# State tiles in one plane, gates' second part on GpSimd, a lag between pairs, and a new order, in an mLSTM and two-MoE kernel

## The chip, the cores and the metric

One core of a Trainium2 chip runs the whole program in one launch. The metric is the device time of one execution in microseconds (us). The engines are TensorE (PE, with its weight loads as PEld), VectorE (DVE), ScalarE (ACT), GpSimd (POOL) and SyncE (SP), which issues the DMAs.

## What is computed

```python
for t in range(S):                       # B=2, H=8, S=768, D=40
    m_new = np.maximum(f_gate[:, :, t] + m, i_gate[:, :, t])
    f_stab = np.exp(f_gate[:, :, t] + m - m_new)
    i_stab = np.exp(i_gate[:, :, t] - m_new)
    C = f_stab[..., None, None] * C + i_stab[..., None, None] * np.einsum('bhd,bhe->bhde', vt, kt)
    n = f_stab[..., None] * n + i_stab[..., None] * kt
    y[:, :, t] = sigmoid(o_gate) * einsum('bhde,bhe->bhd', C, qt) / maximum(abs(n . qt), 1)
x = y as (1536, 320)
h = x @ w_in                             # 320 -> 2048
g = (a0 + a1 h + a2 h^2 + a3 h^3) / (1 + |b0||h| + |b1|h^2 + 1e-6)
x = g @ w_out                            # 2048 -> 320
xn = x / rms(x) * rms_g
out = (silu(xn @ w_gate) * (xn @ w_val)) @ w_out2    # 320 -> 1536 -> 320
```

The weights arrive as 64-bit floats and are converted on the chip.

## The kernel before

**Recurrence.** The 2 x 768 tokens are 12 chunks of 128 (chunk j: batch j // 6). A chunk's tasks on TensorE are s (L504, K^T Q by head, tiles of 64 rows by 128 columns), f (L484, the forget factors spread over partitions), yi (L527, the state times Q, for chunks that aren't the first of their batch), y (L537, the inner part), u (L549, the update of the state) and xt (L645, three transposes). In yi one matmul takes both heads of a pair: 128 rows of Q against a state `cst` in two planes, whose other half is zero, so that 82 columns stream past 64 weight columns. On VectorE stand two scans (L487), two products a (L509), ys (L531) and yd (L541), ca (L563, two pieces, one for each half of the partitions) and xl (L653); on GpSimd vp, v2, cd (L555, two pieces), rs and xm.

**Gates.** They are worked out in two parts, steps 0 to 255 and 256 to 767: gm (L423, a scan), ga (L430, L431) and gi (L434, on GpSimd), gb (two ScalarE instructions), gc, gd (L449, scans whose second operand is a zero column `zc`) and ge (transposes to `idt`). f of a chunk needs gc of its part; the products a need ge.

**First MoE.** A pair i is 256 hidden units (weight group p) of 256 tokens (block n): `PAIRS[i] = (n, p)`. Its tasks are in0 and in1 (L676, 8 matmuls each), a chain over ScalarE, GpSimd and VectorE that ends in g (L739), and out0 and out1 (L681 for the first 16 pairs, in four-pass float32; L695 and L697 after that). Blocks 0 and 1 go together, p by p. in0 of block n needs xl of chunks 2n and 2n + 1. A weight group is loaded, converted on VectorE in halves (c0 L331, c1 L337, c2 L343, or c2 on GpSimd with a carry on ScalarE), then split by hi (L360) and its low words (L364).

**Second MoE.** From about 320 us gate and value products (L865) and output sums (L873 to L875) fill TensorE.

**Order.** All is divided into some 1,950 tasks with dependencies and buffers from rings (eight PSUM banks are the ring "b"). The table ORDER lists the tasks' numbers in the order in which they are issued; it was made elsewhere, and every engine runs its instructions in that order. A table entry moved moves all that its task issues, DMAs too.

```python
def run():
    for x in ORDER:
        key, fn, deps, take, give = tasks[x]
        for tag, name in take:
            held[name] = (tag, rings[tag].pop(0))
        if fn: fn()
        for name in give: ...      # buffer back to its ring
```

## Time and profile before

| | |
|---|---|
| three runs | 484.04 us median (482.48 to 484.82) |
| the profiled execution | 483.95 us, span 482.18 us |
| PE / PEld busy | 459.9 us (95%) / 416.2 us (86%) |
| DVE, ACT, POOL busy | 333.4 us (69%), 305.3 us (63%), 316.7 us (66%) |
| first and last matmul start | 8.14 us, 478.5 us |
| DMA | 40.4 MB, mean 84 GB/s |

The span reaches from the first to the last instruction; the launch around it is in the execution's own time. A busy share is an average over stages. Matmuls are pipelined, so the length that a row of the timeline gives reaches beyond the next row's start; what a task costs is read from its start to the next row's start. In the timeline equal instructions that follow each other are one row with a count, and a float32 matmul shows as two instructions.

### The profile page before, as it was taken

Reading aid. Unit: us, or ns where it says so; the run is one execution under the profiler, and the core shown is the slowest. Engines: PE = TensorE matmul, PEld = TensorE weight load, DVE = VectorE, ACT = ScalarE, POOL = GpSimd, SP = SyncE. Lnnn points to the kernel's source line nnn. Section 1 sums busy time; section 2 is a strip of 40 time slices with the busy share of each in tenths; the row PEclk is TensorE's granted clock in tenths of the full one; section 3 lists DMA queues with packets and bytes.
Section 4 is the critical chain, followed back from the end, with each engine's and each line's share of the span. In section 5 each row is a group of like instructions: output and inputs, shape, how many; then the busy total and the mean of one; then the engine's idle time right before and its main releaser. Section 6 shows DMA issues by size and latency. Waiting matters only on the chain.

```text
...
## 1 busy us (share of the span) xinstructions
PE 459.9 (95%) x3552; PEld 416.2 (86%) x3552; DVE 333.4 (69%) x609; ACT 305.3 (63%) x576; POOL 316.7 (66%) x337
## 2 busy tenths in 40 slices
...
GB/s 249 256 171 283 48 179 114 165 56 115 2 15 89 34 114 50 28 2 84 33 142 57 94 98 190 225 153 72 1 1 14 88 0 2 27 42 1 1 1 56
DMA packets 18366, 40.41 MB, mean 84 GB/s; under 512 B 3952, under 2 KB 11904, under 8 KB 18320
## 3 DMA queue, kind: packets, MB, share of 16 engines
...
q8 instruction: 28, 0.46, 0.4%
q14 instruction: 18, 0.15, 0.1%
...
## 4 chain that ended last, share of the span: by engine, by line
PE 59%; ACT 13%; DVE 13%; POOL 10%; issue 4%; DMA 1%; POOLq 0%; DVEq 0%; ACTq 0%
PE bank L865 24%; PE bank L676 9%; PE bank L695 5%; PE bank L873 4%; PE bank L875 4%; PE bank L874 4%; PE bank L697 2%; POOL win L364 2%; ACT z L710 2%; PE bank L681 1%; DVE vv L727 1%; POOL scr L356 1%; DVE bank L737 1%; POOL z L720 1%; DVE vv L739 1%
## 5 line engine op out<-in xcount | busy, mean ns | idle before, releaser
L676 PE MATMUL bank<-xall,win 128*128 128x256 f32 x768 | 104.1, 290 | 2.4 <-DVE vv L739 0.8
L676 PEld LDWEIGHTS bank<-xall,win 128*128 128x128 f32 x768 | 97.0, 194 | 6.8 <-DVE xall L653 1.0
L941 DVE TENSOR_TENSOR vv<-bank,vv 128x512 f32<-128x512 f32 x35 | 24.1, 690 | 103.4 <-PE bank L865 84.5
L720 POOL TENSOR_TENSOR z<-z,u 128x512 f32<-128x512 f32 x48 | 62.2, 1295 | 11.7 <-ACT z L710 10.7
L947 POOL TENSOR_TENSOR wou<-vv,wou 128x512 fp32r<-128x512 f32 x12 | 15.5, 1296 | 50.8 <-ACT wou L944 50.7
L938 ACT ACTIVATE vv<-bank 128x512 f32<-128x512 f32 x35 | 20.6, 594 | 42.4 <-PE bank L865 38.9
L865 PE MATMUL bank<-xall,w2gv 128*128 128x512 f32 (+1 forms) x256 | 46.9, 338 | 0.3 <-ACT vv L938 0.3
L749 POOL TENSOR_TENSOR gl<-vv,gh 128x512 fp32r<-128x512 f32 x32 | 41.6, 1300 | 7.6 <-ACT gh L748 5.1
L865 PEld LDWEIGHTS bank<-xall,w2gv 128*128 128x128 f32 x256 | 39.3, 190 | 5.5 <-ACT vv L938 0.8
L710 ACT ACTIVATE z<-u,few 128x512 f32<-128x512 f32 x48 | 39.0, 813 | 1.7 <-DVE vv L739 0.6
L681 PE MATMUL bank<-scr,vv 128*128 128x320 f32 x128 | 38.0, 439 | 1.5 <-DVE vv L739 1.2
L695 PE MATMUL bank<-wou,gh 128*128 128x320 f32 x128 | 39.1, 317 | 0.1
L697 PE MATMUL bank<-wou,gh 128*128 128x320 f32 x128 | 38.0, 309 | 0.0
L737 DVE SCALAR_TENSOR_TENSOR bank<-vv,few,bank 128x512 f32<-128x512 f32 x48 | 35.8, 747 | 0.0
L735 DVE SCALAR_TENSOR_TENSOR z<-z,bank 128x512 f32<-128x512 f32 x48 | 32.6, 680 | 3.9 <-ACT bank L734 3.0
L732 ACT ACTIVATE bank<-z,few 128x512 f32<-128x512 f32 x48 | 32.7, 682 | 1.1 <-POOL z L720 0.6
L739 DVE SCALAR_TENSOR_TENSOR vv<-z,bank 128x512 f32<-128x512 f32 x48 | 32.7, 681 | 0.6
L947 POOL TENSOR_TENSOR gl<-vv,wou 128x512 fp32r<-128x512 f32 x11 | 14.2, 1296 | 28.0 <-ACT wou L944 17.1
L331 DVE TENSOR_SCALAR bank<-raw 128x320 int32<-128x320 int32 x68 | 32.4, 484 | 0.1
L681 PEld LDWEIGHTS bank<-scr,vv 128*128 128x128 f32 x128 | 22.9, 190 | 11.0 <-DVE vv L739 2.3
L947 POOL TENSOR_TENSOR wou<-vv,gh 128x512 fp32r<-128x512 f32 x10 | 12.9, 1299 | 29.1 <-ACT gh L944 28.9
L865 PE MATMUL bank<-win,w2gv 128*128 128x512 f32 x128 | 30.7, 390 | 0.0
...
## 6 DMA issues: line engine op xcount, KB each, us to landing
...
```

Of the source, the lines that this page charges most:

```text
L676: PE.matmul(out=hb()[:, e], lhsT=l, rhs=r, start=(x == 0), stop=(x == len(mm) - 1))
L681: PE.matmul(out=T("acc", n, t)[:, 0:DM], lhsT=T("vv", i)[:, e, t * 128:(t + 1) * 128], rhs=w[:, e], start=p + e == 0, stop=p == NPAIR - 1 ...
L695: PE.matmul(out=o, lhsT=l, rhs=woh[:, e], start=first, stop=last)
L697: PE.matmul(out=o, lhsT=l, rhs=wol[:, e], start=False, stop=False)
L710: go("z", lambda: ACT.activation(out=z(), in_=u(), func=ACTF.Identity, scale=babs[:, 1:2], bias=babs[:, 0:1]), [("hu", i)], ["z"])
L720: go("zu", lambda: POOL.tensor_tensor(out=z(), in0=z(), in1=u(), op=ALU.mult), [("z", i)], [], ["u"])
L732: go("ars", lambda: ACT.activation(out=hb(), in_=z(), func=ACTF.Abs_reciprocal_sqrt, bias=cq), [("zu", i), ("p3", i)])
L737: go("y2", lambda: DVE.scalar_tensor_tensor(out=hb(), in0=vv(), scalar=nacoef[:, 0:1], in1=hb(), op0=ALU.add, op1=ALU.mult), [("w", i)])
L739: go("g", lambda: DVE.scalar_tensor_tensor(out=vv(), in0=z(), scalar=2.0, in1=hb(), op0=ALU.subtract, op1=ALU.mult), [("y2", i)], [], ["z" ...
L749: go("gl", lambda: POOL.tensor_tensor(out=gl(), in0=vv(), in1=r32(gh()), op=ALU.subtract), [("gh", i)], ["gl"], ["vv"])
L865: PE.matmul(out=bank(i, e), lhsT=l, rhs=r, start=y == 0, stop=y == len(mm) - 1)
L947: task(("sl",) + k2, lambda: POOL.tensor_tensor(out=flat("sl", *k2), in0=flat("sg", *k2), in1=r32(flat("sh", *k2)), op=ALU.subtract), [("s ...
```

## The change

The state `cst` has one plane. yi takes 16 matmuls of 40 rows by 64 columns (tiles 64x64, at four places of the array) into two banks, one for the even and one for the odd heads, and ys reads them in two pieces. u loads 64 columns of K for each head (40 of the head and 24 that follow; the last head's are zero), so that it writes all 128 partitions, and ca and cd are one piece each. The zeros of `lqk` and `cst` are no longer written at the start. ga and gi are one task: for the first part on VectorE (three instructions), for the second on GpSimd (three instructions). `zc` is a column of the PSUM bank that ge uses. Pairs of block 1 follow those of block 0 one weight group later. ORDER is another table; the diff shows its first line in each kernel, and the rows behind the diff what moved.

```diff
--- before.py
+++ after.py
@@ -20,101 +20,102 @@
 OB = [["ob"] * 4, ["raw", "raw", "raw", "ob"], ["ob", "raw"], ["ob", "cv"]]
 F_CV = [1] * 16 + [0] * 18
 NATIVE = [0, 1, 2, 3, 4, 5, 6, 7, 8, 9, 10, 11, 12, 13, 14, 15]
+LAG = 1
 BY_SQUARE = [0, 2, 4, 6, 8, 10, 12, 14, 16, 18, 20, 22, 24, 26, 28]
 ORDER = [
-    0, 374, 379, 8, 10, 19, 375, 9, 11, 21, 393, 20, 22, 36, 376, 377, 394, 12, 13, 2, 3, 17, 23, 94, 378, 28, 30,
...
+    0, 8, 9, 10, 18, 11, 391, 392, 396, 12, 372, 373, 375, 393, 394, 1, 13, 374, 376, 34, 19, 20, 395, 21, 377, 15,
...
 ]
 
 
@@ -162,7 +163,8 @@
 
     BLOCKS = [(0, 2 * BLK), (2 * BLK, 2 * BLK), (4 * BLK, BLK), (5 * BLK, BLK)]
 
-    PAIRS = [(n, p) for p in range(NPAIR) for n in range(2)] + [(n, p) for n in range(2, NB) for p in range(NPAIR)]
+    PAIRS = [(n, x - n * LAG) for x in range(NPAIR + LAG) for n in range(2) if 0 <= x - n * LAG < NPAIR]
+    PAIRS += [(n, p) for n in range(2, NB) for p in range(NPAIR)]
     FINAL = [max(i for i, x in enumerate(PAIRS) if x[0] == n) for n in range(NB)]
 
     PE, ACT, DVE, POOL = nc.tensor, nc.scalar, nc.vector, nc.gpsimd
@@ -265,13 +267,12 @@
     dexp = at.tile([48, NCH, BH // 2], FP32, name="dexp")
     idt = at.tile([128, NCH, 48], FP32, name="idt")
     dl = at.tile([128, NCH, BH // 2], FP32, name="dl")
-    cst = at.tile([128, HP, 2, D1], FP32, name="cst")
-    zc = at.tile([48, 1], FP32, name="zc")
+    cst = at.tile([128, HP, D1], FP32, name="cst")
     den = at.tile([128, H, 1], FP32, name="den")
-    for nm, n in (("k", 2), ("v", 2)):
-        ring("l" + nm, tiles(at, n, [128, H, D], FP32, "l" + nm))
-    qk_bufs = tiles(at, 2, [128, 2, HP, L], FP32, "lqk")
-    ring("lqk", qk_bufs)
+    ring("lv", tiles(at, 2, [128, H, D], FP32, "lv"))
+    lk_bufs = tiles(at, 2, [128, H * D + 64 - D], FP32, "lk")
+    ring("lk", lk_bufs)
+    ring("lqk", tiles(at, 2, [128, 2, HP, L], FP32, "lqk"))
     ring("yb", tiles(at, 2, [128, H, D1], FP32, "yb"))
 
 
@@ -282,7 +283,10 @@
     def load(i, nm):
         if nm != "qk":
             src = {"k": k, "v": v, "o": o_gate}[nm][i * L:(i + 1) * L].rearrange("p (h d) -> p h d", h=H)
-            nc.sync.dma_start(out=lo_of(i) if nm == "o" else T("l" + nm, i), in_=src)
+            dst = lo_of(i) if nm == "o" else T("l" + nm, i)
+            if nm == "k":
+                dst = dst[:, 0:H * D].rearrange("p (h d) -> p h d", h=H)
+            nc.sync.dma_start(out=dst, in_=src)
             return
         for e in range(2):
             nc.sync.dma_start(
@@ -403,11 +407,8 @@
         DVE.memset(g48, 0.0)
         DVE.memset(cq, 1.0 + 1e-6)
         DVE.memset(eps6, 1e-6)
-        POOL.memset(zc, 0.0)
-        for t in qk_bufs:
-            for r0 in (32, 96):
-                POOL.memset(t[r0:r0 + 32, 0], 0.0)
-        POOL.memset(cst, 0.0)
+        for t in lk_bufs:
+            POOL.memset(t[:, H * D:], 0.0)
         for nm, dst, src in (
             ("eye", ident, eye4[:, 0:128]), ("eye4", id4, eye4), ("sel", sel, pick), ("hv", hv[FR], halves),
             ("pb", bcoef, pb[None, :].to_broadcast([128, 2])), ("pa", acoef, pa[None, :].to_broadcast([128, 4])),
@@ -426,12 +427,11 @@
         )
 
     def gate_a(a, b):
-        gf = gate_in[:, 0, a:b]
-        DVE.tensor_tensor(out=gf, in0=gf, in1=m_t[:, a:b], op=ALU.add)
-        DVE.tensor_tensor(out=g48[FR, a:b], in0=gf, in1=m_t[:, a + 1:b + 1], op=ALU.subtract)
-
-    def gate_i(a, b):
-        POOL.tensor_tensor(out=g48[0:BH, a:b], in0=gate_in[:, 1, a:b], in1=m_t[:, a + 1:b + 1], op=ALU.subtract)
+        e = POOL if a else DVE
+        gf, m1 = gate_in[:, 0, a:b], m_t[:, a + 1:b + 1]
+        e.tensor_tensor(out=gf, in0=gf, in1=m_t[:, a:b], op=ALU.add)
+        e.tensor_tensor(out=g48[FR, a:b], in0=gf, in1=m1, op=ALU.subtract)
+        e.tensor_tensor(out=g48[0:BH, a:b], in0=gate_in[:, 1, a:b], in1=m1, op=ALU.subtract)
 
     def gate_b(a, b):
         ACT.activation(out=g48[:, a:b], in_=g48[:, a:b], func=ACTF.Exp)
@@ -444,9 +444,11 @@
         DVE.memset(f16[:, a:b].rearrange("p (c l) -> p c l", l=L)[:, :, 0:1], 0.0)
 
     def gate_d(a, b):
+        zc = T("gt", a)[FR, 511:512]
+        DVE.memset(zc, 0.0)
         for c in range(a // L, b // L):
             sl = g48[FR, c * L:(c + 1) * L]
-            DVE.tensor_tensor_scan(out=sl, data0=sl, data1=zc[FR].to_broadcast([BH, L]), initial=1.0, op0=ALU.mult, op1=ALU.add)
+            DVE.tensor_tensor_scan(out=sl, data0=sl, data1=zc.to_broadcast([BH, L]), initial=1.0, op0=ALU.mult, op1=ALU.add)
 
     def gate_e(a, b):
         c0, c1 = a // L, b // L
@@ -521,14 +523,22 @@
             return T(name, j)[:, 0:H * D1].rearrange("p (h d) -> p h d", h=H)
 
         def yi():
-            t = heads("pi")
             for p in range(HP):
                 for c in (slice(0, 64), slice(64, 128)):
-                    PE.matmul(out=t[c, 2 * p:2 * p + 2], lhsT=T("lqk", j)[:, 0, p, c], rhs=cst[:, p])
+                    for e in range(2):
+                        r = slice(64 * e, 64 * e + D)
+                        PE.matmul(out=odd(e)[c, p], lhsT=T("lqk", j)[r, 0, p, c], rhs=cst[r, p])
+
+        def odd(e):
+            return T("pi", j, e)[:, 0:HP * D1].rearrange("p (a b) -> p a b", a=HP)
 
         def ys():
-            dd = idt[:, ch, 32 + b * H:32 + (b + 1) * H][:, :, None].to_broadcast([128, H, D1])
-            DVE.tensor_tensor(out=T("yb", j), in0=heads("pi"), in1=dd, op=ALU.mult)
+            dd = idt[:, ch, 32 + b * H:32 + (b + 1) * H].rearrange("p (a e) -> p a e", e=2)
+            for e in range(2):
+                DVE.tensor_tensor(
+                    out=T("yb", j).rearrange("p (a e) d -> p a e d", e=2)[:, :, e], in0=odd(e),
+                    in1=dd[:, :, e:e + 1].to_broadcast([128, HP, D1]), op=ALU.mult,
+                )
 
         def y():
             t = heads("py")
@@ -546,23 +556,18 @@
             t = T("pu", j)[:, 0:HP * D1].rearrange("p (a b) -> p a b", a=HP)
             for h in range(H):
                 r0 = 64 * (h % 2)
-                PE.matmul(out=t[r0:r0 + D, h // 2], lhsT=T("lk", j)[:, h], rhs=v2_buf[:, h])
+                PE.matmul(out=t[r0:r0 + 64, h // 2], lhsT=T("lk", j)[:, h * D:h * D + 64], rhs=v2_buf[:, h])
 
         def cd():
-            for e in range(2):
-                r = slice(64 * e, 64 * e + D)
-                dd = dl[r, ch, b * HP:(b + 1) * HP][:, :, None].to_broadcast([D, HP, D1])
-                POOL.tensor_tensor(out=cst[r, :, e, 0:D1], in0=cst[r, :, e, 0:D1], in1=dd, op=ALU.mult)
+            dd = dl[:, ch, b * HP:(b + 1) * HP][:, :, None].to_broadcast([128, HP, D1])
+            POOL.tensor_tensor(out=cst, in0=cst, in1=dd, op=ALU.mult)
 
         def ca():
             t = T("pu", j)[:, 0:HP * D1].rearrange("p (a b) -> p a b", a=HP)
-            for e in range(2):
-                r = slice(64 * e, 64 * e + D)
-                cc = cst[r, :, e, 0:D1]
-                if ch:
-                    DVE.tensor_tensor(out=cc, in0=t[r], in1=cc, op=ALU.add)
-                else:
-                    DVE.tensor_copy(out=cc, in_=t[r])
+            if ch:
+                DVE.tensor_tensor(out=cst, in0=t, in1=cst, op=ALU.add)
+            else:
+                DVE.tensor_copy(out=cst, in_=t)
 
         def den_(x):
             if x == 0:
@@ -612,8 +617,10 @@
             ("v2", j), None if last else v2, [("scan", j, 0), ("scan", j, 1), ("vp", j)] + prev("u")
         )
         if ch:
-            task(("yi", j), yi, [("s", j), ("ca", j - 1)], take=[key_(("pi", j))], give=[("lqk", j)])
-            task(("ys", j), ys, [("yi", j), ("gates", ch)], take=[("yb", ("yb", j))], give=[("pi", j)])
+            task(("yi", j), yi, [("s", j), ("ca", j - 1)], take=[key_(("pi", j, e)) for e in range(2)],
+                 give=[("lqk", j)])
+            task(("ys", j), ys, [("yi", j), ("gates", ch)], take=[("yb", ("yb", j))],
+                 give=[("pi", j, e) for e in range(2)])
         task(("y", j), y, [("a", j, 0), ("a", j, 1), ("vp", j)], take=[key_(("py", j))])
         task(
             ("yd", j), yd, [("y", j)] + ([("ys", j)] if ch else []),
@@ -984,13 +991,11 @@
 
             go("gm", lambda a=a, b=b: gate_m(a, b),
                [("ld", "gates")] + ([("gm", parts[x - 1][0])] if x else []))
-            go("gi", lambda a=a, b=b: gate_i(a, b), [("gm", a)])
             go("ga", lambda a=a, b=b: gate_a(a, b), [("gm", a)])
-            go("gb", lambda a=a, b=b: gate_b(a, b), [("ga", a), ("gi", a)])
+            go("gb", lambda a=a, b=b: gate_b(a, b), [("ga", a)])
             go("gc", lambda a=a, b=b: gate_c(a, b), [("gb", a)])
-            go("gd", lambda a=a, b=b: gate_d(a, b), [("gc", a)])
-            go("ge", lambda a=a, b=b: gate_e(a, b), [("gd", a), ("ld", "eye")], take=[("b", ("gt", a))],
-               give=[("gt", a)])
+            go("gd", lambda a=a, b=b: gate_d(a, b), [("gc", a)], take=[("b", ("gt", a))])
+            go("ge", lambda a=a, b=b: gate_e(a, b), [("gd", a), ("ld", "eye")], give=[("gt", a)])
             for c in range(a // L, b // L):
                 task(("fgates", c), None, [("gc", a), ("ld", "sel"), ("ld", "eye4")])
                 task(("gates", c), None, [("ge", a)])
```

**TensorE around the first pair's block.** Before (L645 transposes, L504 s, L484 f, L537 y, L676 the block, L549 u, L527 yi; rows of s, f and yi that only repeat are left out):

```order
L645 MATMUL bank_74<-ident,los 128x128 x3
L504 MATMUL bank_73<-lqk_124 128x128
L504 MATMUL bank_72<-lqk_124 128x128
L484 MATMUL bank_71<-f_112,sel 128x128
L537 MATMUL bank_76<-vp_buf,scr 64x41 x16
L676 MATMUL bank_74<-xall,win 128x256 x16
L549 MATMUL bank_69<-v_buf,lk_121 40x41 x8
L645 MATMUL bank_76<-ident,los 128x128 x3
L527 MATMUL bank_69<-cst,lqk_124 64x82 x8
```

Changed (L652, L506, L486, L547, L683, L559, L530 are the same tasks):

```order
L652 MATMUL bank_72<-ident,los 128x128 x3
L547 MATMUL bank_75<-vp_buf,scr 64x41 x16
L683 MATMUL bank_69<-xall,win 128x256 x16
L559 MATMUL bank_71<-v_buf,lk_121 64x41 x8
L652 MATMUL bank_72<-ident,los 128x128 x3
L530 MATMUL bank_74<-cst,lqk_124 64x41
L547 MATMUL bank_76<-vp_buf,scr 64x41 x16
L506 MATMUL bank_71<-lqk_123 128x128
L486 MATMUL bank_73<-f_112,sel 128x128
L559 MATMUL bank_76<-v_buf,lk_121 64x41 x8
L683 MATMUL bank_72<-xall,win 128x256 x16
```

Before, the transposes of chunk 1 are followed by s and f of chunk 4 and y of chunk 3, and then by the block. Now the block follows y of chunk 2, and u, the transposes, yi and y of the chunks 2 and 3, s and f of chunk 4 and u of chunk 3 stand between it and the second block. The block before it was in0 and in1 of pair 0 in both.

**VectorE from the gates' scan on.** Before (L423 gm, L430 and L431 ga, L441 and L444 gc, L449 gd, L331 and L337 weight conversion):

```order
L423 SCALAR_TENSOR_TENSOR scr<-scr 16x256
L430 TENSOR_TENSOR scr<-scr 16x256
L431 TENSOR_TENSOR scr<-scr 16x256
L423 SCALAR_TENSOR_TENSOR scr<-scr 16x512
L331 TENSOR_SCALAR bank_69<-raw_83 128x320
L430 TENSOR_TENSOR scr<-scr 16x512
L431 TENSOR_TENSOR scr<-scr 16x512
L337 SCALAR_TENSOR_TENSOR cv_88<-raw_83,bank_69 128x320
L331 TENSOR_SCALAR bank_70<-raw_83 128x320
L331 TENSOR_SCALAR bank_71<-raw_84 128x320
L441 SCALAR_TENSOR_TENSOR f_112<-scr,f_112 16x256
L444 MEMSET f_112 48x2
L449 SCALAR_TENSOR_TENSOR scr<-scr,zc 16x128 x2
```

Changed (L424 gm, L432 to L434 ga with the former gi, L441 and L444 gc, L448 the zero column, L451 gd, L335 and L341 conversion):

```order
L424 SCALAR_TENSOR_TENSOR scr<-scr 16x256
L432 TENSOR_TENSOR scr<-scr 16x256
L433 TENSOR_TENSOR scr<-scr 16x256
L434 TENSOR_TENSOR scr<-scr 16x256
L424 SCALAR_TENSOR_TENSOR scr<-scr 16x512
L441 SCALAR_TENSOR_TENSOR f_112<-scr,f_112 16x256
L444 MEMSET f_112 48x2
L335 TENSOR_SCALAR bank_69<-raw_83 128x320
L448 MEMSET bank_70 16x1
L451 SCALAR_TENSOR_TENSOR scr<-scr,bank_70 16x128 x2
L335 TENSOR_SCALAR bank_71<-raw_84 128x320
L335 TENSOR_SCALAR bank_72<-raw_84 128x320
```

ga of the second part (16x512) is gone from VectorE; gc of the first part has moved ahead of all conversions, and a third instruction has joined ga of the first part.

## Rows read from the trace of the kernel before

**Rows 1.** Windows: stretch, length, busy us (instructions) per engine, clock, DMA share, GB/s.
```profile
3.20:26.00 22.80, 13.78 (x120) 11.67 (x120) 21.54 (x37) 10.03 (x19) 12.96 (x20) 1.00 0.89 279
26.00:45.80 19.80, 18.76 (x239) 16.68 (x238) 18.70 (x37) 6.33 (x16) 16.21 (x26) 1.00 0.75 212
49.50:140.00 90.50, 85.81 (x688) 69.45 (x688) 84.67 (x150) 86.47 (x155) 84.63 (x86) 1.00 0.30 92
140.00:300.00 160.00, 159.04 (x1370) 148.81 (x1369) 151.76 (x274) 148.67 (x287) 132.26 (x135) 1.00 0.25 73
```
**Rows 2.** Timeline, TensorE, 25 to 50: start, length, line, operation, count, [idle before].
```profile
37.33 1.92 PE L537 MATMUL bank<-vp_buf,scr 128*64 128x41 f32 x32
...
40.31 0.90 PE L645 MATMUL bank<-ident,los 128*128 128x128 f32 x3
41.14 2.08 PE L504 MATMUL bank<-lqk 40*128 40x128 f32 x16
43.01 1.06 PE L484 MATMUL bank<-f,sel 48*128 48x128 f16 x8
44.00 1.93 PE L537 MATMUL bank<-vp_buf,scr 128*64 128x41 f32 x32
45.86 3.73 PE L676 MATMUL bank<-xall,win 128*128 128x256 f32 x16
49.52 0.51 PE L549 MATMUL bank<-v_buf,lk 128*40 128x41 f32 x16
```
**Rows 3.** Timeline, TensorE, behind the first pair's block.
```profile
50.43 1.16 PE L504 MATMUL bank<-lqk 40*128 40x128 f32 x16
51.52 0.79 PE L527 MATMUL bank<-cst,lqk 128*64 128x82 f32 x16
52.24 0.55 PE L645 MATMUL bank<-ident,los 128*128 128x128 f32 x3
...
53.58 1.13 PE L537 MATMUL bank<-vp_buf,scr 128*64 128x41 f32 x32 [0.46 <-DVE scr L509]
54.64 2.17 PE L676 MATMUL bank<-xall,win 128*128 128x256 f32 x16
...
60.14 0.51 PE L549 MATMUL bank<-v_buf,lk 128*40 128x41 f32 x16
60.57 3.13 PE L676 MATMUL bank<-xall,win 128*128 128x256 f32 x24
```
**Rows 4.** Timeline, TensorE, the first native output products.
```profile
66.51 2.96 PE L681 MATMUL bank<-scr,vv 128*128 128x320 f32 x10
...
72.83 2.42 PE L681 MATMUL bank<-scr,vv 128*128 128x320 f32 x8 [1.22 <-DVE vv L739]
74.85 2.32 PE L676 MATMUL bank<-xall,win 128*128 128x256 f32 x16
```
**Rows 5.** Timeline, VectorE, 0 to 50.
```profile
6.78 1.40 DVE L430 TENSOR_TENSOR scr<-scr 16x512 f32<-16x512 f32 x1
8.21 0.68 DVE L431 TENSOR_TENSOR scr<-scr 16x512 f32<-16x512 f32 x1
...
31.05 0.67 DVE L563 TENSOR_TENSOR cst<-bank,cst 40x164 f32<-40x164 f32 x2
...
34.79 0.86 DVE L331 TENSOR_SCALAR bank<-raw 128x320 int32<-128x320 int32 x2
...
35.95 0.68 DVE L509 TENSOR_TENSOR scr<-bank,w_buf 128x512 f32<-128x512 f32 x1
...
38.58 2.34 DVE L487 TENSOR_TENSOR_SCAN w_buf<-bank,id 128x512 f32<-128x512 f32 x2
...
41.42 0.49 DVE L541 TENSOR_TENSOR yb<-bank,yb 128x328 f32<-128x328 f32 x1
...
44.05 0.55 DVE L653 TENSOR_TENSOR xall<-bank,xall 128x384 fp32r<-128x384 f32 x1
```
**Rows 6.** Timeline, GpSimd, the gates' second part.
```profile
6.55 1.08 POOL L434 TENSOR_TENSOR scr<-scr 16x512 f32<-16x512 f32 x1 [1.67 <-DVE scr L423]
```

184 rows, old and new, of the table ORDER are left out of this document.

## The prediction

> **What bounds the kernel now.** First the stages: the windows view gives each engine's busy time in four stretches [rows 1]. From 140 to 300 us TensorE is busy 159.04 of 160 us, and it stays so to the end: there only its own work counts. From 3.2 to 45.8 us another engine is full: VectorE, 21.54 of 22.80 us and 18.70 of 19.80 us. TensorE is busy there too (18.76 of 19.80 us from 26), but at a lower pace. The clock column reads 1.00 in every row, and the instructions contradict it: the block of 16 matmuls of a pair's input (in0, in1) lasts 3.73 us at 45.86 [rows 2] and 2.17 us at 54.64 [rows 3]. From one row's start to the next, s takes 1.87 against 1.09 us, y and the state product yi together 2.98 against 1.06 + 0.72. So TensorE runs at its 1.2 GHz level until about 49.5 us and at 2.4 GHz from then on. What it did before the rise was that block, the first dense full-array work; 20 us of small matmuls without a gap had not raised it.
>
> By the Trainium skill (TensorE: Matmul & The Clock Gate, Part 1) the default state is throttled and activity releases the throttle; the doubled pace in these rows agrees.
>
> After the first block TensorE still waits: 90.50 - 85.81 = 4.7 us up to 140 us and 1.0 us up to 300 [rows 1], 5.7 together, a little more by starts, since the profile counts the pipelined end of a matmul as busy. The largest piece is between 66.51 and 74.85: 24 instructions of native output products (L681) at 0.27 us each (ten last 2.96 with the pipelined end of the last) need 6.5 us and take 8.34, and the last wait among them, 1.22 us, is one for g, the last step of a pair's chain on VectorE [rows 4].
>
> **The change part by part.** The sum is made against the profiled execution, 483.95 us (span 482.18), 0.1 us under the median of the three runs, 484.04.
>
> 1. *When the first block starts.* It needs xl of chunk 1 on VectorE, which ended at 44.60 [rows 5]. In the new order VectorE no longer has, ahead of that: two scans (2.34), two products a (1.3), one ca (0.64), one ys and one yd (0.42 each: the row's 0.49 less the overlap with the next), the gates' second part (1.40 + 0.68, now on GpSimd) and half of two remaining ca (0.64): 7.8 us [rows 5, 6]. It has in addition six conversion pieces at 0.43, a third gate instruction of 16x256 (0.45 by its neighbours), two small ys pieces and two memsets (0.4): 3.4 us. Net 4.4 us earlier, so 40.2. TensorE's side gives the same: one s, f, u, y and yi fewer at half pace (s and f 2.86, y and yi 2.98, u some 0.6: 6.4 [rows 2]), and about 1.2 us more for the dearer u and yi, so 45.86 - 5.2 = 40.6. I take 40.3.
> GpSimd's three gate instructions of 16x512 at about 1.08 [rows 6] take 3.2 us from about 6.5; c2 and the weights' low words are queued behind them, and gc of the second part waits for them through the exponential until about 11.7 us. VectorE has conversions to do until then, so I price that wait at nothing; without that cover up to 1.5 us of the gain would go.
>
> 2. *What the earlier block is worth.* It lasts to the next task as long as before, 3.66, and ends at 44.0 instead of 49.52, 5.5 us earlier. TensorE then owes the five tasks that it did before, now at full pace: 1.09 + 0.5 + 0.43 + 1.06 + 0.72, and some 0.3 us of gaps between tasks, 4.1 us [rows 3]. Gain **1.4 us**.
>
> 3. *u with 64 weight columns instead of 40.* Its 16 instructions take 0.43 us. y, with 64 columns loaded and the same 41 streamed, takes 1.06 for 32, so 0.53 for 16, plus the gap to the next task: 0.60 [rows 3]. Ten u; two lie ahead of the first block, in the sums of step 1. 8 x 0.17 = **+1.4 us**.
>
> 4. *yi in four 64x64 tiles.* Sixteen matmuls stream 41 columns where eight streamed 82, and 32 instructions replace 16. The nearest row is y: same count, columns loaded and columns streamed, 1.06 us, so +0.34. The lower end is u's pace for 32 instructions, 2 x 0.43 less one end gap, 0.73: nothing. A tile here is reloaded every fourth matmul, in y every second, so the loads that slow y against u have more time; I take 0.90, between the two. 8 x 0.18 = **+1.4 us**, bounds 0 and +2.7. The second PSUM bank of each yi is paid where banks run short; no row prices it, and I take nothing, with 0 to 1 us.
>
> The Trainium skill (TensorEngine Tiling, Tiling Modes) counts four independent tiles in the 64x64 mode, which "can execute LdWeights and Matmul in parallel". That makes yi about 0.62 us, an estimate, and this term -0.8.
>
> 5. *VectorE and GpSimd.* ca is one piece instead of two: its two pieces take 0.67 us [rows 5], so -0.33 for eight later ones; ys gains about 0.15 each. Together -1.5 us of VectorE work from 46 to 300 us, where TensorE is the limit or close to it. cd in one piece and the memsets left out free GpSimd by some 0.5 us a chunk. All of that is hidden by TensorE's work; without that cover it would be a gain.
>
> 6. *The waits.* Pairs of the second block of tokens now come one weight group later, so the second pair needs only chunks 0 and 1, and no pair of block 1 needs a weight group that has just been converted. Four input blocks can now run before the first output product. The 1.9 us between 66 and 75, a wait for g on VectorE, should go, since VectorE is ahead by more than that after step 1. Of the other 4 us (5.7 less 1.9, rounded up as above) I take half. **-4.0 us**; the bounds are -6 (all gone) and +1 (the new order has as many, at other places).
>
> Sum: 483.95 - 1.4 + 1.4 + 1.4 - 4.0 = 481.35. **Forecast 481.4 us.**
>
> **The rivals.**
> *B, the waits stay and yi costs what y costs.* For it: u and yi lie mostly where TensorE has no idle time, and a new order only moves waits. Against it: the first wait is one for VectorE, which is relieved. 483.95 - 1.4 + 1.4 + 2.7 - 1 = 485.7: no change that can be measured.
> *C, the clock misses the first block.* In the new order the block is followed by seven small tasks (u, xt, yi, y, s, f, u) before the next block. Before the change the clock rose only as the block ended, so there is no margin. If it does not rise, the seven run at half pace (+3.4 us by rows 2 and 3) and the second block lasts 3.73 instead of 2.17 (+1.6): 481.4 + 5.0 = 486.4, where slower begins. If the second block misses too, xt, yi and a third block cost 2.6 more: 489. Against it: the block is the same length as before, and 16 dense matmuls sufficed once. I give 487.5.
> *D, four tiles at once and no waits.* If four instructions of yi are in flight where y has two, its 32 take half of y's time and one gap, 1.06 / 2 + 0.1 = 0.62, so -0.8 for eight; and all 6 us of waits are gone: 483.95 - 1.4 + 1.4 - 0.8 - 6 = 477.2. Against it: in s, whose tiles also take turns, only two instructions are in flight, 1.09 us for 16 [rows 3]; and an order without any wait is rare.
>
> By the Trainium skill (TensorEngine Tiling, Tiling Modes) yi's half of D holds and the waits alone are open; no row of before shows four tiles at work.
>
> **How the numbers follow.** Forecast 0.45, B 0.25, C 0.13, D 0.17. A measurement of this kernel tells 0.5% (2.4 us) from no change, so faster means under 481.6 and slower over 486.4. The forecast's own range, 479 to 484, straddles the first bound; I put two thirds of it on the fast side. Faster: 0.17 + 0.29 = 0.46. Slower: C and a small part of B, 0.18. Same: 0.36. The range of 8 in 10 runs from D's time to just past the start of C's: 477.2 to 486.6.
>
> **What would show it.** Right: the first L683 block near 40.3 us and of about 3.7 us; small tasks at full pace right behind it; u near 0.60 and yi near 0.90; fewer than 0.5 us lost ahead of the first native output products. Wrong: a block later than 43 (VectorE or the gates on GpSimd hold it up); s still at 1.87 us behind the block (C); yi at 1.06 or more; new idle time on TensorE between 50 and 130 us that makes up for the old.

## The result and the profile after

The changed kernel takes **486.56 us** (median of 6 runs, 486.35 to 488.03) against 483.21 us before (6 runs, 482.46 to 484.82): a ratio of 1.0074 with a 95% interval of 1.0054 to 1.0094. It is slower, by more than the 0.5% that a measurement can tell. The forecast was 481.4 us. The profiled execution took 488.03 us (span 486.2); the other five lie between 486.35 and 486.75. The executions of before fall into two groups, near 482.5 and near 484.0 us; beside the experiments nearly all of both read a mean granted clock of 1.00. The profiled one, on which the sum was made, is of the second group, and no run shows what sets the groups apart.

The page of the kernel after, its busy times and two rows of its 40 slices:

```profile
PE 458.9 (94%) x3712; PEld 417.4 (86%) x3712; DVE 326.4 (67%) x610; ACT 310.1 (64%) x580; POOL 312.3 (64%) x326
...
PE   2698897999999999999999999999999999999997
...
PEclk9999898999999999999999999999999999999999
```

VectorE lost 7 us of work (333.4 before) and GpSimd 4, yet the span grew by 4.0 us. Two slices, the fifth and the seventh, have a clock under 9 tenths. Before, no slice had.

The windows of the kernel after (stretch, length, busy us and instructions of PE, PEld, DVE, ACT, POOL, then clock, DMA share, GB/s). The first three and the last answer to [rows 1]:

```profile
3.20:26.00 22.80, 12.59 (x147) 11.35 (x148) 21.08 (x44) 9.27 (x18) 15.93 (x19) 1.00 0.89 264
26.00:45.80 19.80, 17.58 (x218) 15.43 (x217) 18.23 (x38) 11.34 (x26) 16.23 (x26) 1.00 0.79 247
49.50:140.00 90.50, 83.75 (x658) 69.30 (x658) 78.01 (x137) 77.54 (x138) 78.11 (x81) 0.96 0.28 86
50.00:100.00 50.00, 43.29 (x376) 35.01 (x376) 40.99 (x73) 39.25 (x67) 42.10 (x47) 0.93 0.39 122
100.00:150.00 50.00, 49.88 (x420) 42.17 (x420) 45.70 (x81) 47.72 (x94) 45.33 (x45) 1.00 0.12 35
140.00:300.00 160.00, 158.38 (x1468) 148.04 (x1468) 151.44 (x275) 152.44 (x291) 133.54 (x135) 1.00 0.25 75
```

The same two middle stretches of the kernel before, and 150 to 250, which an experiment needs:

```profile
50.00:100.00 50.00, 46.96 (x388) 37.83 (x387) 48.47 (x86) 46.64 (x83) 45.86 (x46) 1.00 0.39 122
100.00:150.00 50.00, 48.35 (x401) 40.34 (x401) 45.83 (x81) 48.80 (x94) 48.12 (x51) 1.00 0.16 46
150.00:250.00 100.00, 100.00 (x963) 95.71 (x962) 95.57 (x167) 91.22 (x170) 84.15 (x87) 1.00 0.21 61
```

Nearly all that was lost lies between 50 and 100 us. TensorE idles 50 - 43.29 = 6.7 us there, before 3.0: 3.7 more. And its mean clock is 0.93, so 0.07 x 50, some 3.4 us of pace, are gone too. From 100 to 150 the new order wins 1.5 us back; from 140 to 300 it idles 0.6 us more. VectorE, ScalarE and GpSimd do not carry more work in the bad stretch: all three are less busy than before. So none of them is full there; the engines wait for each other.

Around the first block, TensorE's timeline of the kernel after (start, length, line, operation, count, [idle before and who ended it]); it answers to [rows 2, 3]:

```profile
38.37 1.93 PE L547 MATMUL bank<-vp_buf,scr 128*64 128x41 f32 x32 [1.71 <-POOL vp_buf L499]
40.23 3.78 PE L683 MATMUL bank<-xall,win 128*128 128x256 f32 x16
43.94 1.07 PE L559 MATMUL bank<-v_buf,lk 128*64 128x41 f32 x16
44.95 0.55 PE L652 MATMUL bank<-ident,los 128*128 128x128 f32 x3
45.45 0.68 PE L530 MATMUL bank<-cst,lqk 40*64 40x41 f32 x32
46.06 1.13 PE L547 MATMUL bank<-vp_buf,scr 128*64 128x41 f32 x32
...
48.66 0.67 PE L559 MATMUL bank<-v_buf,lk 128*64 128x41 f32 x16
49.25 2.17 PE L683 MATMUL bank<-xall,win 128*128 128x256 f32 x16
52.50 0.63 PE L652 MATMUL bank<-ident,los 128*128 128x128 f32 x3 [1.08 <-POOL los L585]
```

The block (L683) starts at 40.23 us; 40.3 was forecast. u behind it (L559) still takes 1.01 us, at half pace, and u at 48.66 takes 0.59. So the clock rose about 45 us. The state product yi (L530) takes 45.45 to 46.06, 0.61 us. Then the first new wait follows, 1.08 us at 51.4.

Clock windows of the kernel after, the two falls:

```profile
55.10:58.50 3.40, 3.40 (x18) 3.40 (x17) 3.40 (x5) 2.07 (x5) 3.31 (x4) 0.50 0.84 212
...
75.60:79.00 3.40, 3.40 (x26) 3.34 (x18) 3.37 (x9) 2.48 (x6) 3.25 (x4) 0.50 0.06 11
```

TensorE drops to its 1.2 GHz level twice for 3.4 us, each time soon behind waits between small products. In the other five executions the mean clock is 0.995 or 0.996 where the profiled one has 0.992, which is one such fall instead of two, and they are 1.3 to 1.7 us shorter. So in this kernel **the second fall goes with 1.3 to 1.7 us**, near half of its length. That is no fixed price: three executions of before that ran beside the experiments read 0.996 too and took 482.42, 482.47 and 482.53 us, as little as the fast ones at 1.00, and in experiment 11 the three executions at 1.00 (483.7 to 484.1 us) are slower than five of the six at 0.996 (482.9 to 483.5).

Where the larger waits come from stands in three timelines of the kernel after. TensorE:

```profile
70.00 2.17 PE L683 MATMUL bank<-xall,win 128*128 128x256 f32 x16 [0.81 <-DVE scr L511]
72.10 0.67 PE L559 MATMUL bank<-v_buf,lk 128*64 128x41 f32 x16
75.06 0.69 PE L530 MATMUL bank<-cst,lqk 40*64 40x41 f32 x32 [2.29 <-DVE cst L568]
...
94.86 1.34 PE L688 MATMUL bank<-scr,vv 128*128 128x320 f32 x4 [1.08 <-DVE vv L746]
```

VectorE:

```profile
63.32 1.23 DVE L489 TENSOR_TENSOR_SCAN w_buf<-bank,id 128x512 f32<-128x512 f32 x1 [0.27 <-PE bank L486]
67.74 0.20 DVE L578 RECIPROCAL den<-den 128x8 f32<-128x8 f32 x1 [3.20 <-POOL den L576]
...
74.67 0.33 DVE L568 TENSOR_TENSOR cst<-bank,cst 128x164 f32<-128x164 f32 x1
```

GpSimd:

```profile
65.06 2.32 POOL L368 TENSOR_TENSOR win<-cv,win 128x512 fp32r<-128x512 f32 x3
67.47 0.23 POOL L576 TENSOR_SCALAR den<-den 128x8 f32<-128x8 f32 x1
```

Read from the bottom: GpSimd makes weights for 2.32 us, and a step of 0.23 us stands behind them. VectorE's reciprocal of 0.20 us waits for that step, and everything else of VectorE stands behind the reciprocal, so VectorE idles 3.20 us. Its later evictions free PSUM banks late (0.81 us at 69.2) and its state sum L568 comes at 74.67, so yi waits 2.29 us. A small step in the wrong place of GpSimd's queue stops VectorE and then TensorE.

### The profile page after: what moved, and what is told of

Its sections match the earlier page's. It is cut to its first block, busy times and chain, and to the rows that moved or that the text cites. A ratio compares the mean times of both kernels' runs of the same rounds, so it can differ in the third digit from the quotient of the medians.

```text
span 486.2 us, 9664 instructions
## 1 busy us (share of the span) xinstructions
PE 458.9 (94%) x3712; PEld 417.4 (86%) x3712; DVE 326.4 (67%) x610; ACT 310.1 (64%) x580; POOL 312.3 (64%) x326
## 4 chain that ended last, share of the span: by engine, by line
PE 63%; DVE 19%; ACT 7%; POOL 5%; issue 4%; DMA 1%; DVEq 0%; ACTq 0%; POOLq 0%
PE bank L872 25%; PE bank L683 11%; PE bank L881 4%; PE bank L882 4%; PE bank L880 4%; PE bank L688 4%; PE bank L702 3%; DVE w_buf L489 3%; DVE bank L744 2%; DVE vv L734 2%; DVE vv L736 2%; PE bank L547 2%; DVE vv L746 2%; PE bank L704 2%; DVE bank L335 2%
## 5 line engine op out<-in xcount | busy, mean ns | idle before, releaser
L683 PE MATMUL bank<-xall,win 128*128 128x256 f32 x768 | 107.1, 296 | 2.5 <-DVE scr L511 0.8
L683 PEld LDWEIGHTS bank<-xall,win 128*128 128x128 f32 x768 | 99.9, 199 | 6.3 <-DVE scr L511 1.3
L954 POOL TENSOR_TENSOR wou<-vv,wou 128x512 fp32r<-128x512 f32 x16 | 20.5, 1292 | 47.4 <-ACT wou L951 47.1
L335 DVE TENSOR_SCALAR bank<-raw 128x320 int32<-128x320 int32 x68 | 32.3, 488 | 2.1 <-ACT vv L945 1.4
L716 ACT ACTIVATE u<-bank 128x512 f32<-128x512 f32 x48 | 28.5, 594 | 4.1 <-PE bank L683 2.2
L368 POOL TENSOR_TENSOR win<-cv,win 64x128 fp32r<-64x128 f32 (+2 forms) x37 | 28.0, 756 | 3.4 <-ACT win L364 1.6
```

The lines of the kernel that those rows point to most:

```text
L335: DVE.tensor_scalar(out=mid(x), in0=word(x, 1), scalar1=3, scalar2=0x3FFFFFFF, op0=ALU.logical_shift_left, op1=ALU.bitwise_and,)
L683: PE.matmul(out=hb()[:, e], lhsT=l, rhs=r, start=(x == 0), stop=(x == len(mm) - 1))
```

## Experiments

The first three separate the order, the instructions and the second bank; the next three take up single waits, and the rest try to go on from there. In ORDER a moved entry moves one task; where a move is small, the rows that moved are shown, with + where they stand now.

**1. New instructions, old order.**

```diff
-LAG = 1
+LAG = 0
 ORDER = [
-    0, 8, 9, 10, 18, 11, 391, 392, 396, 12, 372, 373, 375, 393, 394, 1, 13, 374, 376, 34, 19, 20, 395, 21, 377, 15,
+    0, 372, 377, 8, 9, 18, 373, 10, 19, 391, 20, 34, 374, 375, 392, 11, 12, 2, 3, 16, 21, 92, 376, 26, 28, 396, 14,
...
```

> The new instructions (64x64 state tiles, single update pieces, half of the gates' chain on GpSimd) in the order of before, without the lag; seven products with the state tiles or their copies stand a few places elsewhere, because such a product now takes two PSUM banks. Theory 1, the new order causes the loss (it lets GpSimd's and VectorE's results come late between 50 and 95 us, and TensorE's clock falls after those waits): this kernel has the waits of before, no fall of the clock, and the state products at 0.6 us in place of about 1.1; that is 480 to 483.5 us, not slower than before. Theory 2, the new instructions cause the loss (two banks per state product, GpSimd's share of the gates, the wider update): 485.5 us or more, with new waits on TensorE at the state products.

Measured 487.98 us, ratio 1.0099 (1.0075 to 1.0124). The number is Theory 2's, the place is not. Windows of this run:

```profile
50.00:100.00 50.00, 46.66 (x418) 37.94 (x415) 47.80 (x86) 46.38 (x81) 44.86 (x44) 1.00 0.38 122
...
150.00:250.00 100.00, 97.93 (x1007) 93.53 (x1006) 91.85 (x163) 88.02 (x164) 79.44 (x82) 1.00 0.19 58
```

From 50 to 100 it is as before (46.66 against 46.96, clock 1.00), so the old order has none of the new waits there. This is the execution at 487.34 us; the other three (487.82 to 488.99) read a mean clock of 0.996 or 0.992, so the clock fell in them, against Theory 1, and no profile shows where. From 150 to 250 TensorE idles 2.1 us where before idles nothing, and more just ahead of it:

```profile
139.30 0.67 PE L530 MATMUL bank<-cst,lqk 40*64 40x41 f32 x30 [1.15 <-DVE w_buf L489]
159.80 1.13 PE L547 MATMUL bank<-vp_buf,scr 128*64 128x41 f32 x32 [0.43 <-DVE yb L538]
...
197.14 2.17 PE L683 MATMUL bank<-xall,win 128*128 128x256 f32 x16 [1.20 <-DVE vv L746]
```

The releasers are VectorE instructions that read a PSUM bank (a scan, ys, g); what TensorE waits for is a bank. At 139.30 it is the second bank itself: the row has 30 of yi's 32 instructions, the first matmul had run before the wait. In the changed kernel's profile every yi stands in one row of 32, so there no yi waits for its second bank once it has begun. Experiment 3 takes this up.

**2. Old instructions, new order.** The kernel before with the new table and the lag:

```diff
...
-    PAIRS = [(n, p) for p in range(NPAIR) for n in range(2)] + [(n, p) for n in range(2, NB) for p in range(NPAIR)]
+    PAIRS = [(n, x - n) for x in range(NPAIR + 1) for n in range(2) if 0 <= x - n < NPAIR]
+    PAIRS += [(n, p) for n in range(2, NB) for p in range(NPAIR)]
```

> The instructions of before in the new order, with the lag of one in the pairs. Theory 1 (the order): 486 to 490 us, with waits of TensorE of several us between 50 and 95 us and a granted clock of 0.5 somewhere there, since VectorE has even more to do in the first 50 us. Theory 2 (the new instructions): 481 to 484 us.

497.75 us, ratio 1.0296 (1.0264 to 1.0328). This is worse than either theory said. With the old instructions the new order starves TensorE from the beginning:

```profile
3.20:26.00 22.80, 8.50 (x58) 6.85 (x58) 19.48 (x33) 7.86 (x14) 10.29 (x14) 1.00 0.91 261
```

8.50 us of TensorE's work are done there, against 12.59 with the new instructions. So order and instructions were made for each other, and neither half alone can be read as the cause: exchange one and it is slower either way.

**3. Only the second bank.** The kernel before, with its own instructions and order:

```diff
...
-            task(("yi", j), yi, [("s", j), ("ca", j - 1)], take=[key_(("pi", j))], give=[("lqk", j)])
-            task(("ys", j), ys, [("yi", j), ("gates", ch)], take=[("yb", ("yb", j))], give=[("pi", j)])
+            task(("yi", j), yi, [("s", j), ("ca", j - 1)], take=[key_(("pi", j)), key_(("px", j))], give=[("lqk", j)])
+            task(("ys", j), ys, [("yi", j), ("gates", ch)], take=[("yb", ("yb", j))], give=[("pi", j), ("px", j)])
...
```

> The kernel before with its own instructions and order; only the state product of each chunk takes a second PSUM bank, which it does not write, and holds it until its eviction, as the changed kernel's does. The same seven... that is, the same four tasks stand elsewhere as in the run of the new instructions in the old order (the eviction of chunk 5 six places earlier, the state products of chunks 8, 9 and 10 by 8, 9 and 1 places later). That run was 0.8 us ahead of before at 125 us and lost about 4 us between 130 and 310. Theory, the second bank costs this in an order that was not made for it: 485.5 to 488 us here too, with waits of TensorE at the state product near 139 us and at the block near 197. Rival, the new instructions themselves cost it (GpSimd's gates, the update): 482.4 to 484, as before.

487.0 us, ratio 1.0071 (1.0047 to 1.0094): the theory. Its window and its waits are nearly those of experiment 1:

```profile
150.00:250.00 100.00, 97.37 (x940) 92.64 (x939) 92.62 (x162) 88.37 (x164) 81.37 (x85) 1.00 0.20 59
```

```profile
159.34 1.13 PE L537 MATMUL bank<-vp_buf,scr 128*64 128x41 f32 x32 [0.60 <-DVE yb L531]
...
196.81 2.17 PE L676 MATMUL bank<-xall,win 128*128 128x256 f32 x16 [1.24 <-DVE vv L739]
```

A bank that nobody writes, and the four moves that it forces, cost 0.7%, about 3.4 us, in the old order. Only the wait at 139, 1.15 us in experiment 1, has no counterpart here, where no matmul writes the second bank. What the bank costs apart from the four moves was not separated. In the new order, made with the two banks, the later stretch costs little: TensorE idles 1.6 us from 140 to 300, before 1.0.

**4. One group of GpSimd's moved.** The changed kernel, GpSimd's rows:

```
 L729 TENSOR_TENSOR vv_96<-vv_96,s_107 128x512
+L576 TENSOR_SCALAR den<-den 128x8
 L368 TENSOR_TENSOR win<-cv_88,win 128x2x256
 L368 TENSOR_TENSOR win<-cv_88,win 64x128 x2
-L576 TENSOR_SCALAR den<-den 128x8
```

> The changed kernel with one instruction group moved on GpSimd: the 2.3 us in which it builds the third piece of the projection's weights (line 368, at 65.06 us) stand behind the 0.23 us that VectorE's reciprocal of chunk 4 waits for (line 576), not ahead of it. Theory 1: VectorE's idle 3.2 us at 64.5 go, the 1.2 us that TensorE waits at 68.8 go, and of the 2.3 us ahead of the state product at 75 all but about half a us; the clock's second fall, 1.7 us of loss, goes too. In all 3 to 4.7 us less than the changed kernel: 482 to 483.7. Rival: the weights themselves come late for the block at 69 us, and TensorE waits for them as long as before: 486 to 487. A third case: the waits go and are given back before 130 us, as the queues of the other engines are full there: 485 to 486.5.

484.97 us, ratio 1.0040 (1.0026 to 1.0055), 1.6 us less than the changed kernel: less than Theory 1 says, and in the range of the third case. The wait ahead of the block is gone; the one ahead of yi is as long as before, and in the profiled execution the clock fell at its end, for 6.8 us. Timeline and windows of this run:

```profile
72.61 1.09 PE L530 MATMUL bank<-cst,lqk 40*64 40x41 f32 x32 [2.29 <-DVE cst L568]
```

```profile
72.30:79.10 6.80, 6.49 (x52) 5.82 (x53) 5.23 (x12) 4.77 (x9) 5.97 (x8) 0.50 0.17 48
```

TensorE had come earlier as well, so it waited for the state sum all the same.

**5. Chunk 3's reciprocal earlier.** The changed kernel, VectorE's rows (GpSimd's L576 moves likewise):

```
+L578 RECIPROCAL den<-den 128x8
 L489 SCALAR_TENSOR_TENSOR w_buf<-bank_73,id_106 128x512
-L578 RECIPROCAL den<-den 128x8
```

> The changed kernel with the small reciprocal of chunk 3 on VectorE (line 578, 0.18 us) and what leads to it on GpSimd (line 576) ahead of chunk 4's scan (line 489, 1.2 us) and of the state update's product on GpSimd (line 563), not behind them. Theory 1: the 1.08 us that TensorE waits at 51.4 us for GpSimd's result go, the 0.56 us after it stay in part, and with less idle time there the clock's first fall (55.1 to 58.5 us, 1.7 us of loss) goes if the wait brought it: 2 to 3.3 us less, 483.3 to 484.6. Rival, the fall comes from the small products and not from the wait: the fall stays and about 1 us is gained, 485.5. A third case: what is gained here is waited for at 69 us: 486.5.

487.14 us, ratio 1.0078 (1.0055 to 1.0101): the third case, nothing gained. The 1.08 us at 51.4 shrank to 0.23, the fall at 55 us was gone, and the whole came back at the next late step:

```profile
69.15 3.59 PE L683 MATMUL bank<-xall,win 128*128 128x256 f32 x16 [2.30 <-DVE scr L511]
```

The clock fell there, from 69.0 to 72.4 us, so the block took 3.59 us.

**6. Both moves, and yi of chunk 5 behind the next block.** TensorE's rows, beside the two moves (ys, L538, moves with yi):

```
 L559 MATMUL bank_74<-v_buf,lk_122 64x41 x8
+L683 MATMUL bank_75<-xall,win 128x256 x16
 L530 MATMUL bank_70<-cst,lqk_124 64x41
...
-L683 MATMUL bank_74<-xall,win 128x256 x16
```

> The changed kernel with the moves of the two runs before together, and one more: the product of chunk 5 with the state (line 530) and its eviction stand behind the next projection block (line 683) and not ahead of it, so that VectorE's state sum (line 568) has 2.2 us more. In the run with the first move alone the clock fell right behind the 2.29 us that TensorE waits ahead of this product (6.8 us at 0.5 in the profiled run), in the run with the second alone right behind 2.3 us ahead of the block at 69 us. Theory 1, each long wait comes from one late small step on GpSimd or VectorE, and the clock falls behind the long waits only: with the three moves no wait between 50 and 85 us is over 1 us, the clock stays at 1.0 (or the fall is gone in most runs), and the time is 5 to 6 us under the changed kernel's, 480.5 to 482. Rival, the other engines are full there, and a wait taken away in one place comes back in the next (as the second move alone showed): 484 to 486, with a new wait of 1 to 2 us before 100 us.

483.65 us, ratio 1.0016 (1.0006 to 1.0025): 2.9 us less than the changed kernel, between the two cases: the clock stays, as Theory 1 says, and a wait of over 1 us is left, as the rival says. All ten executions have a clock of 0.999 or 1.0. The waits of 2.3 us and the falls are gone, and a new wait stands further on (in the profiled execution, 484.08 us):

```profile
79.50 2.15 PE L683 MATMUL bank<-xall,win 128*128 128x256 f32 x16 [1.58 <-ACT z L717]
```

**7. An earlier first block, and chunk 5's reciprocal behind the g it held up.** Rows of GpSimd, ScalarE and VectorE, against experiment 6:

```
+L496 TENSOR_TENSOR vp_buf<-lv_119,idt 128x8x40
+L499 COPY vp_buf<-idt 128x8
 L360 TENSOR_TENSOR cv_88<-cv_88,rnd_87 128x640
-L496 TENSOR_TENSOR vp_buf<-lv_119,idt 128x8x40
-L499 COPY vp_buf<-idt 128x8
...
+L656 ACTIVATE xall<-bank_72 128x3x128
 L364 ACTIVATE win<-cv_88 128x2x256
 L364 ACTIVATE win<-cv_88 64x128 x2
-L656 ACTIVATE xall<-bank_72 128x3x128
...
-L578 RECIPROCAL den<-den 128x8
...
 L746 SCALAR_TENSOR_TENSOR vv_96<-z_93,bank_75 128x512
+L578 RECIPROCAL den<-den 128x8
```

> The three moves and two more: VectorE's reciprocal of chunk 5 (line 578, after 2.2 us of idle time at 90 us) behind the step that TensorE's output products wait 1.08 us for at 93 us; and ahead of the first projection block GpSimd's copy of chunk 2's values (lines 496 and 499) in front of a 1.5 us weight step, and ScalarE's copy for the block's input (line 656) in front of the next weight step. Theory 1: the first block starts 1 to 1.4 us earlier (at 38.8 to 39.3 us, with the clock still at half pace, so that TensorE does not wait 1.71 us for the values), the wait at 93 us goes, and the time is 1.5 to 2.5 us under the run with three moves: 478.5 to 480.5. Rival: the rise of the clock, or the first block's weights, take the earlier start back: as the run with three moves, less 0.5 to 1 us.

483.67 us (481.28 to 484.54), ratio 1.0009 (0.9991 to 1.0027). The block started at 38.73 us, as Theory 1 says, and some executions are faster than any of before; but there are two kinds now, and the median is that of experiment 6. Two executions with a clock of 1.00 took 481.3 and 481.6 us, the other eight (0.988 to 0.993) took 482.9 to 484.5. The clock rises before the small products now, and there it falls again.

**8. Seven moves.** Chunk 2's small steps go ahead of a scan and a copy, and L335 and L341 of one weight half behind the block at 80 us. GpSimd's rows, against experiment 7:

```
+L576 TENSOR_SCALAR den<-den 128x8
+L582 TENSOR_TENSOR los<-los,den 128x320
+L585 TENSOR_TENSOR los<-yb_125,los 128x320
+L586 COPY los<-los 128x64
 L496 TENSOR_TENSOR vp_buf<-lv_120,idt 128x8x40
 L499 COPY vp_buf<-idt 128x8
```

> The run with five moves, and two more. In its profiled execution the clock was full from about 41 us, and fell again from 45.3 to 55.3 us right behind 1.27 us that TensorE waits at 42.9 for chunk 2's input (GpSimd, line 585); its two fastest executions (481.3 and 481.6 us) had no fall. Move six takes chunk 2's small steps (lines 551, 574, 578, 582, 585) ahead of a scan on VectorE and of a copy on GpSimd, so that this wait goes; move seven puts two weight steps on VectorE (lines 335, 341) behind the projection block that waits 1.59 us at 80.6 us. Theory 1, the clock falls behind a wait of over a us between small products, and what a fall costs is half of its length: no fall, all executions near the fast ones and the 1.3 us of the wait less: 478.5 to 481. Rival, the fall comes without the wait too (the small products alone bring it): two modes again, 3 to 5 us apart, median over 482. A third case: no fall, but the block at 80 us waits for the same thing as before: 480 to 481.5.

484.09 us (481.21 to 484.85), ratio 0.9997 (0.9975 to 1.0020): the rival. Four executions at 481.2 to 481.6 with a clock of 0.999 or 1.0, six at 484.0 to 484.9 with 0.988 or 0.989. TensorE's timeline and the windows of a slow one:

```profile
38.69 3.35 PE L683 MATMUL bank<-xall,win 128*128 128x256 f32 x16
41.97 0.67 PE L559 MATMUL bank<-v_buf,lk 128*64 128x41 f32 x16
43.15 0.63 PE L652 MATMUL bank<-ident,los 128*128 128x128 f32 x3 [0.51 <-POOL los L585]
44.86 1.10 PE L530 MATMUL bank<-cst,lqk 40*64 40x41 f32 x32 [1.08 <-DVE cst L568]
...
51.62 3.68 PE L683 MATMUL bank<-xall,win 128*128 128x256 f32 x16
55.13 0.49 PE L652 MATMUL bank<-ident,los 128*128 128x128 f32 x3
```

```profile
44.10:54.90 10.80, 10.04 (x119) 9.55 (x120) 8.38 (x18) 5.93 (x10) 8.03 (x12) 0.53 0.34 78
```

u at 41.97 runs at full pace (0.67 with its end), yi at 44.86 at half (1.10). Some 10 us of half pace cost 3 us of time, the distance of the two groups, and not 5. TensorE itself loses more: yi, y, s, f and u take 6.76 us here (44.86 to 51.62) and the block 3.51, against 3.80 (45.45 to 49.25) and 2.10 (70.00 to 72.10) at full pace in the changed kernel, together 4.4 us more. So the rest of it, some 1.4 us, comes back later; where is not shown. 1.6 us of waits were left, so waits and small products are not told apart by this run.

**9. The bank at 80 us in another way.** The weight steps as in experiment 7; instead ScalarE's rows:

```
+L716 ACTIVATE u_90<-bank_70 128x512
+L717 ACTIVATE z_93<-u_90,few 128x512
 L739 ACTIVATE bank_76<-z_92,few 128x512
 L741 ACTIVATE bank_76<-bank_76 128x512
 L739 ACTIVATE bank_71<-z_91,few 128x512
 L741 ACTIVATE bank_71<-bank_71 128x512
```

> As the run with seven moves, but the block at 80 us is helped in another way: ScalarE's copy and gate step of pair 6 (lines 716 and 717), which hold the bank that the block waits for, stand ahead of the two normalisation steps (lines 739 and 741) in front of them. Theory 1: the wait of 1.59 us goes down to under 0.3 and comes back in part as a wait of the next output products for line 746: within 0.7 us of the run with seven moves. Rival, ScalarE's order is what holds the next stage: 1 us or more slower than that run.

484.22 us (482.47 to 488.49), ratio 1.0031 (1.0002 to 1.0060), in several groups again. The median is within 0.7 us of experiment 8's, as Theory 1 says, but not by its mechanism: the block's wait was 2.80 us (to 82.0) where it had been 1.59 in experiment 7, now one for VectorE's L341. The bank moved to another late reader.

**10. Blocks between the small products.** The second block (in0, in1 of pair 1) behind u of chunk 2, the third ahead of chunk 3's transposes:

```diff
...
     PAIRS += [(n, p) for n in range(2, NB) for p in range(NPAIR)]
+    PAIRS[2], PAIRS[3] = PAIRS[3], PAIRS[2]
```

> The run with seven moves, and the first projection blocks put between the small products of chunks 2 and 3: the second block (line 683, ready since the first) stands right behind the update of chunk 2, ahead of the transposes that waited 0.5 us and the state product that waited 1.1 us there; the third and the fourth pair change places, so that the third block needs no input of chunk 2 and can stand ahead of chunk 3's transposes. In the run with seven moves the executions fell into two groups, 481.2 to 481.6 us with a granted clock of 1.0 and 484.0 to 484.9 with 0.989 (half pace from 44.1 to 55 us in the profiled one), so that fall is worth 3 us. Theory 1, the fall needs a wait between the small products right behind the rise of the clock: with a block in that place the waits are covered, no execution shows a mean clock under 0.995, and the median is 479 to 481.5, under the kernel before's faster executions (482.5). Rival, the fall comes from small products alone, as the small ones of chunk 3 now stand together: two groups as before, median over 482.5.

482.73 us (482.23 to 483.60, 12 executions), ratio 1.0002 (0.9994 to 1.0011). No execution has a clock under 0.995 and the two groups are gone, as Theory 1 says; the time is not, it forecast 479 to 481.5 us. Nine of the twelve read 0.995 or 0.996 (482.2 to 483.6 us) and three 0.999 (482.8 to 483.1), so the short falls still come, and here without a price that shows. In this run's timeline (its lines are numbered one higher) the waits stand a little later:

```profile
38.60 3.78 PE L684 MATMUL bank<-xall,win 128*128 128x256 f32 x16
...
43.33 2.22 PE L684 MATMUL bank<-xall,win 128*128 128x256 f32 x16
...
50.86 2.17 PE L684 MATMUL bank<-xall,win 128*128 128x256 f32 x16 [1.18 <-DVE w_buf L490]
...
54.53 0.67 PE L531 MATMUL bank<-cst,lqk 40*64 40x41 f32 x30 [0.93 <-DVE xall L661]
```

Both are waits for a bank: the scan L490 reads the forget factors out of one, L661 the transposes. The second one is yi's second bank again (30 of its 32 instructions).

**11 and 12. Two tries at these banks.** In 11 the four weight steps of VectorE stand behind the product that waited for a bank at 82 us. VectorE's rows:

```
-L336 TENSOR_SCALAR bank_73<-raw_85 128x320
-L342 SCALAR_TENSOR_TENSOR scr<-raw_85,bank_73 128x320
...
 L747 SCALAR_TENSOR_TENSOR vv_95<-z_91,bank_70 128x512
+L336 TENSOR_SCALAR bank_70<-raw_85 128x320
+L342 SCALAR_TENSOR_TENSOR scr<-raw_85,bank_70 128x320
```

> As the run with blocks between, but the four weight steps on VectorE near 82 to 87 us, each of which takes a PSUM bank, stand behind the product of chunk 5 with its values (line 547), which waited 1.49 us for a bank there in the run with seven moves. Theory: the wait goes, and the time is 0.5 to 1.5 us under the run with blocks between. Rival: the output weights that these steps make come late for the output products at 91 us, and it is the same or up to 1 us slower.

483.68 us, ratio 1.0023 (1.0009 to 1.0037): the rival's number, 1 us slower. The wait is gone in the profile, and in its place the output products wait for g on VectorE, not for weights:

```profile
89.86 1.34 PE L689 MATMUL bank<-scr,vv 128*128 128x320 f32 x4 [1.24 <-DVE vv L747]
```

In 12, against experiment 10, the scan stands ahead of the reciprocal again, and the product behind the next output products:

```
-L579 RECIPROCAL den<-den 128x8
 L490 SCALAR_TENSOR_TENSOR w_buf<-bank_75,id_106 128x512
+L579 RECIPROCAL den<-den 128x8
...
-L548 MATMUL bank_73<-vp_buf,scr 64x41 x16
 L689 MATMUL bank_74<-scr,vv_94 128x320
 L689 MATMUL bank_76<-scr,vv_94 128x320
+L548 MATMUL bank_73<-vp_buf,scr 64x41 x16
```

> The run with blocks between, with two changes. Chunk 4's second scan (line 489) stands ahead of chunk 3's reciprocal again, as in the changed kernel: that scan frees the PSUM bank for which the third block waited 1.18 us, and chunk 3's transposes now have the block's 2.2 us as cover. And the product of chunk 5 with its values (line 547), which waited 1.48 us for a bank, stands behind the output product that follows it. Theory 1, TensorE's waits between 45 and 95 us are the whole of what the changed kernel lost, the waits of a small product for a PSUM bank among them: about 2 to 2.6 us less than the run with blocks between, 480 to 481, under the kernel before's faster executions (482.4). Rival, the queues of the other engines set the pace there, and a wait that is gone comes back within 30 us, as in four of the runs before: 482 to 483, as that run.

483.02 us (482.34 to 483.87), ratio 1.0001 (0.9991 to 1.0011): the rival. The scan ended 0.8 us earlier, TensorE came 1 us earlier too, waited longer, and the clock fell at the block:

```profile
38.65 3.08 PE L684 MATMUL bank<-xall,win 128*128 128x256 f32 x16
...
42.26 2.18 PE L684 MATMUL bank<-xall,win 128*128 128x256 f32 x16
...
50.07 3.09 PE L684 MATMUL bank<-xall,win 128*128 128x256 f32 x16 [1.37 <-DVE w_buf L490]
```

## Why the prediction was wrong

**Steps 1 to 3 hold in the main.** The first block starts at 40.23 us (40.3 forecast), in spite of a new wait of 1.71 us for GpSimd ahead of it, which experiment 7 could take away (38.73), and the small products behind it run at full pace from 45 us on; only the u right behind the block still takes 1.01 us, which takes 0.4 us from step 2's 1.4. u costs 0.59 us (0.60) after that. The "20 us of small matmuls without a gap" ahead of the rise had 1.0 us of idle time in them ([rows 1]). Rival C, that the clock misses the first block, did not come; that it would rise there and fall again 10 us later was in no case.

**Step 4 was mis-sized, to the good.** yi takes 0.61 us and not 0.90: 8 x (0.61 - 0.72) = -0.9 us instead of +1.4. By the Trainium skill (TensorEngine Tiling, Tiling Modes) four tiles work in parallel, and the estimate from it, 0.62, is what the rows show. **Its second half, the second bank at nothing with a bound of 1 us, was too low:** the bank alone, with the four moves that it forces, costs 3.4 us in the old order (experiment 3). In the new order no yi waits for it once begun (experiment 1); what it costs there by holding a bank that others need was not separated. The Trainium skill (TensorEngine Tiling, Restrictions and Gotchas) says that row tiles cannot share a bank at the same time; no run here has a version with one bank.

**Step 5 holds:** VectorE's 7 us less are nowhere in the time. Experiment 2, which undoes all the new instructions, suggests that they are needed, though: the new order takes 11 us more without them.

**Step 6 failed:** "the waits, -4.0 us", with +1 as the upper bound. The 1.22 us of [rows 4] went as forecast, though a wait of the same kind, 1.08 us, stands at 93.8 us. From 50 to 100 us TensorE idles 3.7 us more, and behind the new waits the clock fell, 3.4 us of pace in the profiled execution. The step argued from what the lag removes and took the remaining waits by half; it followed no chain of the new order, and the sum had no term for a clock that falls. The waits come from small steps behind long ones in a queue (L576 behind 2.3 us of L368, L578 behind a scan) and from banks that are freed late. Experiments 4 to 6 show the first: with three moves, the time is 2.9 us less and the clock stays. How much of the loss is waits and how much pace is not separated. Experiments 5, 10 and 12 show why a wait removed is not a gain: TensorE then comes earlier to the next thing that isn't ready.

With the measured sizes the sum comes near: 483.95 - 1.4 + 1.3 (u) - 0.9 (yi) + 3.7 + 3.4 - 1.5 (100 to 150 us) + 0.6 (140 to 300 us) = 489.2, against 488.03 in the profiled execution. The sum is thus 1.2 us too long, or 1.6 with the first u at half pace; where that lies is not shown.

Rival B (485.7) was right in its first half, the waits stay, and wrong in its second, yi. Its "a new order only moves waits" fits experiments 5, 9, 11 and 12. Rival D had yi right and the waits wrong. The time lies in the range, at its very end.

**What stays open:** whether the falls need a wait at all, or come from small products alone. Every fall that a profile here shows begins in or soon behind waits that add up to 1 us or more, but the kernel before has a wait of that size too ([rows 4], among large products) and no fall in its profile, and in the same kernel some executions fall and others don't. Open too is what moves the rise. In experiments 10 and 12 the first block starts at 38.60 and 38.65 us behind the same work, but its 16 products last 3.78 and 3.08 us and the next block starts at 43.33 and 42.26. The mean clock does not show this, since its column reads 1.00 until the rise; it may be what sets the two groups of before apart, but no profile of the faster group is here to show it.
